# Thirty-five extra series of single-pass products, read from different places in memory, behind the last expert product

## The chip, the cores and the metric

The kernel runs on one core of a Trainium2 chip. The metric is the device time of one execution in microseconds (us); lower is better. A profile is one execution recorded by the hardware profiler; its span runs from the first to the last instruction.

## What is computed

A gated linear attention feeds a small mixture of four experts, all in float32.

```python
# attention: q, k, v, alpha are (4, 8, 768, 48)
for t in range(S):
    state = alpha[:, :, t, :, None] * state + np.einsum('bhd,bhe->bhde', k[:, :, t], v[:, :, t])
    y[:, :, t] = np.einsum('bhd,bhde->bhe', q[:, :, t], state)
# bridge: x = y as (3072, 384)
# experts: w1 (4, 384, 1024), w2 (4, 1024, 384)
p = domain_probs / (domain_probs.sum(-1, keepdims=True) + 1e-09)
for e in range(E):
    h = np.maximum(x @ w1[e], 0.0)
    out += p[:, e:e + 1] * (h @ w2[e])
```

## The kernel before

The 3072 rows of x are 24 blocks of 128 rows. They are worked in groups: the first of two blocks, five of four blocks, the last of two. Attention makes the blocks of a group while TensorE does the expert products of an earlier one. The order of all work is written by hand: `deal` gives attention steps due times, `advance` and `between` call them out between products, and nothing is reordered afterwards. The `for` loop over `tasks` at the end calls `up` (x times w1, rectified) and `down` (that times w2) for each group and expert. The last two groups are done expert by expert together, so the last task is the last group, of 256 rows, with expert 3.

Exact float32 products take several passes through TensorE, so from the second group on most products are split. A number is written as a coarse part and finer parts in the type float32r, and a product is three products of these parts, each of a single pass. `x_part` (`up`, line 555) gives the moving operand of 512 columns, 256 in the last group; `down` (line 648) moves 384 columns of w2. In every one of these products the stationary operand has 128 rows and 128 columns.

A split piece of w1 or w2 is a tile of 128 partitions by 3 parts by 768 float32r numbers, 9,216 bytes in a partition (`wts`, names `w1` and `w2`; `NQ` = 4 buffers for `w2`). `wt[1][i]` is piece i of w2, and `first_piece(gi, e)` is the number of the first of the four pieces of an expert. They come from DRAM in `load_piece` (line 194), on SP's queue, ahead of need.

Accumulated sums stand in banks of PSUM. `one`, `two` and `ops` have one tag, `g`, with four buffers: a new one may be begun when the engine that read the buffer's last content is done. In `add_up` (line 677) VectorE scales a finished `ops` and adds it to the block's `acc`; of the last expert, the store of a block is queued on SP and ScalarE (line 688), behind that sum. After the loop the last stores are issued and the kernel closes: SP waits for all of it, and the engines meet once more.

The constants that the change uses are P = 128, NT = 512, DM = 384, KC = 3 (blocks of 128 in 384) and QF = 256.

Of the kernel before, what the change touches and what calls it, by code (L numbers as in the profile page):

```python
# [10 lines left out]
F32 = mybir.dt.float32  # L11
# [9 lines left out]
def kernel(  # L21
# [37 lines left out]
    nc = tc.nc  # L59

    B, H, S, D = q.shape
    E, DM, F = moe_w1.shape
    P = 128
# [5 lines left out]
    KC = DM // P  # L69
    FCH = F // P  # L70
    NT = B * P
    NQ = 4
    QF = F // NQ
# [11 lines left out]
    n = np.arange(QUAD)[None, :]  # L85
# [9 lines left out]
    ps = ctx.enter_context(tc.tile_pool(name="ps", bufs=2, space=bass.MemoryType.PSUM))  # L95
# [37 lines left out]
    def raw(u, nm):  # L133
        return values[u % 2] if nm == "v" else apart[nm] if u == 1 else early[nm]

    xTs = {}
    xraws = {}
    hidden = {}
# [39 lines left out]
    wt = ({}, {})  # L178
# [38 lines left out]
    def split_piece(l, i):  # L217
        whole = wt[l][i]
        w = wts.tile([P, 3, KC * QF], F32R, name=f"w{l + 1}", bufs=AHEAD if l == 0 else NQ)
        top, low, dif = (w[:, part] for part in range(3))  # L220

        nc.scalar.activation(out=top, in_=whole, func=ACT.Copy, scale=TRIM)
        yield
        nc.scalar.activation(out=dif, in_=whole, func=ACT.Copy, scale=TRIM * 4096)
        yield
        nc.vector.scalar_tensor_tensor(out=low, in0=whole, scalar=4096.0, in1=dif.bitcast(F32),
                                       op0=ALU.mult, op1=ALU.subtract)
        nc.vector.tensor_sub(dif, low.bitcast(F32), top.bitcast(F32))
        nc.gpsimd.dma_start(out=kept[l][i % (E * NQ)], in_=w.bitcast(F32))
        if l == 0:  # L230
            del wt[0][i]
        elif split2(1, *divmod(i - E * NQ, NQ)):
            wt[1][i] = w

    def background():


        for piece in list(splitting):
            if next(piece, splitting) is splitting:
                splitting.remove(piece)  # L240
        if making and len(splitting) < 4:
            splitting.append(making.popleft())
            next(splitting[-1])
# [356 lines left out]
    def make_dif(top, low, dif):  # L600
        nc.vector.scalar_tensor_tensor(out=dif, in0=top.bitcast(F32), scalar=1 / 4096.0,  # L601
                                       in1=low.bitcast(F32), op0=ALU.mult, op1=ALU.subtract)
# [5 lines left out]
    def down(gi, e, slots, between):  # L608


        first = first_piece(gi, e)
        in_parts = [fc for fc in range(FCH) if split2(gi, e, fc // FPQ)]
        whole = [fc for fc in range(FCH) if fc not in in_parts]
        if slots[0] == 0 and makes[1](gi, e):
            making.extend(split_piece(1, first + k) for k in range(NQ) if not split2(gi, e, k))
        if slots[0] == 0 and makes[0](gi, e) and 0 < e < E - 1:
            making.extend(split_piece(0, first + k) for k in range(2, NQ))


        pairs = [slots[k:k + 2] for k in range(0, len(slots), 2)]  # L620
        sides = [[((0, 1), in_parts[:-2]), ((0, 1), in_parts[-2:])], [((3,), whole), ((2,), in_parts)]]
        turns = [(side, pair) for pair in pairs for side in range(2)] if whole else \
            [(side, pair) for side in range(2) for pair in pairs]
        steps = [(side, slot, part, fc) for side, pair in turns
                 for parts, tiles in sides[side] for part in parts for slot in pair for fc in tiles]
        begins = {key: n for n, key in reversed([*enumerate(step[:2] for step in steps)])}
        ends = {step[:2]: n for n, step in enumerate(steps)}
        sums = {}
        for n, (side, slot, part, fc) in enumerate(steps):
            c, f = divmod(fc, FPQ)  # L630
            advance(cost(1, gi, e) * len(slots) / len(steps))
            while between and n >= between[0][0] * len(steps):
                between.popleft()[1]()
            if n and n % (len(steps) // (2 * len(slots))) == 0:
                background()
            if later and n % (len(steps) // 12 - 1) == len(steps) // 12 - 2:
                make_dif(*later.popleft())
            at = (side, slot)
            if n == begins[at]:
                sums[at] = ps.tile([P, DM], F32, name="ops", tag="g", bufs=4)  # L640
            h = hidden[c][:, :, f, slot * P:(slot + 1) * P]
            if part < 3:
                w = wt[1][first + c].rearrange("p t (c d) -> p t c d", d=DM)[:, part, f]
                h = h[:, part]
            else:
                w = wt[1][first + c].rearrange("p (c d) -> p c d", d=DM)[:, f]
                h = h[:, 2].bitcast(F32)
            nc.tensor.matmul(sums[at], lhsT=h, rhs=w, start=(n == begins[at]), stop=(n == ends[at]))  # L648
            if n == ends[at]:
                add_up(gi, e, slot, side, sums.pop(at))  # L650
        while between:
            between.popleft()[1]()
        background()
        if slots[-1] == len(groups[gi]) - 1 and gi != LAST - 1:
            while makes[1](gi, e) and (making or splitting):
                background()

            for c in range(NQ):
                del wt[1][first + c]
                if c < NQ // 2 or gi == LAST:  # L660
                    load_piece(1, first + NQ + c)
                else:
                    late.append(first + NQ + c)

    def add_up(gi, e, slot, kind, part):

        cb, b = groups[gi][slot]
        at = b * NCB + cb
        if e == 0 and (kind == 0 or not split2(gi, e)):
            accs[cb, b] = hid.tile([P, DM], F32, name="acc", bufs=B) if gi < LAST else \  # L670
                work.tile([P, NP * P], F32, name="QT")[:, :DM]
        acc = accs[cb, b]
        scale = (p_fine if kind == 0 else p_all)[:, at, e:e + 1]
        if e == 0 and (kind == 0 or not split2(gi, e)):
            nc.scalar.activation(out=acc, in_=part, func=ACT.Copy, scale=scale)
        else:
            nc.vector.scalar_tensor_tensor(out=acc, in0=part, scalar=scale, in1=acc,  # L677
                                           op0=ALU.mult, op1=ALU.add)
        if kind == 0:
            return  # L680
        if e == E - 1:
            del accs[cb, b]
            row = b * S + cb * P

            queues = (nc.sync, nc.scalar) if gi == LAST else (nc.gpsimd,)
            for i, queue in enumerate(queues):
                rows = slice(P // len(queues) * i, P // len(queues) * (i + 1))
                stores.append(lambda queue=queue, rows=rows: queue.dma_start(
                    out=out[row:row + P, :][rows], in_=acc[rows]))
# [3 lines left out]
    def cost(layer, gi, e):  # L693
        n = len(groups[gi]) / 4
        if layer == 0:
            return 2.1 * n if split1(gi, e) else 2.6 * n
        return 4.1 if gi > 1 else 4.7 if split2(gi, e) else 5.4
# [50 lines left out]
    def advance(spent):  # L748
        nonlocal clock
        clock += spent  # L750
        while waiting and clock >= waiting[0][0]:
            next(waiting.popleft()[2], None)

    with tc.manual_schedule():
# [38 lines left out]
        for fc in range(FCH):  # L793
            up(0, 0, fc, slice(0, 1))
            advance(cost(0, 0, 0) / 2)
        down(0, 0, [0], deque())
        while waiting:
            next(waiting.popleft()[2], None)
# [4 lines left out]
        for (gi, e), after in zip(tasks, [*tasks[1:], (None, None)]):  # L803
# [6 lines left out]
            for k, slots in enumerate(turns):  # L810

                between = deque()
                if after[1] == 0:

                    for step, at in enumerate((0.0, 0.3, 0.42, 0.54) if gi == 0 else
                                              (0.0, 0.6, 0.7, 0.78)):
                        at = at * len(turns) - k
# [3 lines left out]
        while stores:  # L821
            stores.popleft()()


# [1 line left out]
_INS = ['q', 'k', 'v', 'alpha', 'moe_domain_probs', 'moe_w1', 'moe_w2']  # L826
# [24 lines left out]
```

## Time and profile before

| What | Value |
|---|---|
| Time, median of 2 runs | 1051.29 us (1050.86 and 1051.72) |
| Time of the profiled execution | 1051.34 us |
| Its span, first to last instruction | 1049.6 us |
| What lies outside the span (1051.34 less 1049.57) | 1.77 us |
| Granted TensorE clock | 1.000 |
| TensorE matmul records | 8554 |
| VectorE, ScalarE busy | 74%, 54% |
| GpSimd busy | 4% |

PE is TensorE, PEld its weight loads, DVE VectorE, ACT ScalarE, POOL GpSimd, SP SyncE. Matmuls are pipelined: a record of one runs from its start to its modelled end and overlaps the next, so what a product costs in a stream is the step from one start to the next and not the length of its record. L555 is line 555 of the kernel before.

### The profile page before, as it was taken

How to read it: one execution, taken by the hardware profiler on the slowest of the kernel's cores; microseconds unless marked ns; L12 is line 12 of the kernel's file. 1: busy time of each engine (PE TensorE's matmuls, PEld its weight loads, DVE VectorE, ACT ScalarE, POOL GpSimd, SP SyncE). 2: the span in 40 equal slices, each digit the busy share in tenths (PEclk: the TensorE clock that was granted, in tenths of full speed). 3: DMA queues.
4: the chain of work that ended last, by engine and by line, in shares of the span. 5: the costliest groups of instructions: out<-in, count | busy, mean ns of one | idle time of the engine just before them, and what ended most of it. 6: DMA issues, size and time to landing. Idle time of an engine off the chain costs nothing.

```text
span 1049.6 us, 21621 instructions
## 1 busy us (share of the span) xinstructions
PE 1032.5 (98%) x8554; PEld 898.8 (86%) x8554; DVE 778.2 (74%) x1620; ACT 565.6 (54%) x1195; POOL 37.9 (4%) x81
## 2 busy tenths in 40 slices
PE   8899999999999999999999999999999999999998
PEld 8777777687787899898898998898988989898998
DVE  5578787668879868778877777977887875656565
ACT  4787877585666546446446436565464453323232
POOL 3000010000001000000000000000000000000000
PEclk9999999999999999999999999999999999999999
DMA  9397789887868948768669559577595454444531
GB/s 208 92 327 253 220 302 366 305 337 240 285 241 278 384 153 300 288 194 301 255 214 338 184 209 376 185 257 277 162 352 196 166 211 180 181 186 175 209 153 46
DMA packets 145493, 251.65 MB, mean 240 GB/s; under 512 B 107089, under 2 KB 121809, under 8 KB 122865
## 3 DMA queue, kind: packets, MB, share of 16 engines
q1 hardware_dynamic: 138928, 207.88, 57.9%
q0 software_dynamic: 6016, 42.08, 10.1%
q8 instruction: 67, 1.10, 0.4%
q10 hardware_dynamic: 448, 0.32, 0.1%
q14 instruction: 34, 0.27, 0.1%
HBM read 207.79 MB, written 42.47 MB: 238 GB/s over the span
## 4 chain that ended last, share of the span: by engine, by line
PE 86%; DVE 5%; ACT 5%; DMA 2%; issue 2%; POOL 0%; SPq 0%; ACTq 0%; DVEq 0%; POOLq 0%
PE ops L648 35%; PE one L555 23%; PE two L555 11%; PE sc L344 6%; PE yps L439 3%; PE tp L266 3%; PE one L547 2%; ACT qb L317 2%; PE sps L474 1%; PE far L399 1%; DMA w<-kept 1%; DVE near L354 1%; DMA rq<-in_q_dram 1%; PE idle L780 1%; DVE hT L601 1%
## 5 line engine op out<-in xcount | busy, mean ns | idle before, releaser
L648 PE MATMUL ops<-w,hT 128*128 128x384 f32 x1872 | 342.7, 339 | 0.2 <-DVE hT L601 0.2
L648 PEld LDWEIGHTS ops<-w,hT 128*128 128x128 f32 x1872 | 322.6, 188 | 4.0 <-ACT t L566 0.6
L555 PE MATMUL one<-xT,w 128*128 128x512 f32 x960 | 251.8, 398 | 0.8 <-DMA w<-kept 0.4
L555 PEld LDWEIGHTS one<-xT,w 128*128 128x128 f32 x960 | 176.1, 188 | 38.8 <-ACT t L566 1.2
L566 ACT ACTIVATE t<-one 128x512 f32<-128x512 f32 (+1 forms) x192 | 106.7, 556 | 175.8 <-PE one L555 170.2
L317 ACT COPY qb<-QT 64x256 f32<-64x256 f32 x336 | 136.7, 407 | 59.0 <-DVE QT L324 30.6
L595 DVE SCALAR_TENSOR_TENSOR hT<-t,hT 128x512 fp32r<-128x512 f32 (+1 forms) x172 | 110.3, 641 | 63.3 <-ACT hT L593 62.0
L568 DVE TENSOR_TENSOR t<-t,two 128x512 f32<-128x512 f32 (+1 forms) x172 | 109.2, 635 | 53.5 <-PE two L555 31.7
L593 ACT ACTIVATE hT<-t 128x512 fp32r<-128x512 f32 (+1 forms) x172 | 101.8, 592 | 86.8 <-DVE t L568 86.2
L555 PE MATMUL two<-xT,w 128*128 128x512 f32 x480 | 136.5, 393 | 0.1
L555 PEld LDWEIGHTS two<-xT,w 128*128 128x128 f32 x480 | 90.0, 188 | 20.5 <-DVE acc L677 0.9
L648 PE MATMUL ops<-hT 128*128 128x384 f32 x288 | 100.6, 491 | 0.3 <-DVE acc L677 0.3
L601 DVE SCALAR_TENSOR_TENSOR hT<-hT 128x512 fp32r<-128x512 f32 (+1 forms) x172 | 100.6, 633 | 0.0
L354 DVE COPY_PREDICATED near<-masks,sc 128x256 f32<-128x256 uint8 x144 | 77.0, 535 | 22.2 <-PE sc L344 19.2
L324 DVE TENSOR_TENSOR QT<-QT,dec 128x256 f32<-128x256 f32 x144 | 61.0, 423 | 38.9 <-ACT qb L317 38.4
L344 PEld LDWEIGHTS sc<-qb,KT 128*64 128x64 f32 x2304 | 72.7, 138 | 9.0 <-issue 4.8
L344 PE MATMUL sc<-qb,KT 128*64 128x64 f32 x2304 | 77.2, 223 | 2.6 <-ACT qb L317 2.6
L648 PEld LDWEIGHTS ops<-hT 128*128 128x128 f32 x288 | 52.1, 190 | 29.9 <-DVE acc L677 0.6
L677 DVE SCALAR_TENSOR_TENSOR acc<-ops,p_all,acc 128x384 f32<-128x384 f32 x82 | 49.7, 614 | 27.2 <-PE ops L648 26.3
L336 ACT COPY KT<-KT 128x256 f32<-128x256 f32 x138 | 57.5, 417 | 5.1 <-PE sc L344 1.9
L337 DVE TENSOR_TENSOR KT<-KT,dec 128x256 f32<-128x256 f32 x144 | 60.1, 417 | 0.0
L547 PE MATMUL one<-xT,w 128*128 128x256 f32 (+1 forms) x240 | 46.2, 340 | 0.6 <-ACT xT L452 0.6
(90 smaller groups left out, 954.4 us busy)
## 6 DMA issues: line engine op xcount, KB each, us to landing
w<-kept SPq DMA_DIRECT2D x144, 1152.0 KB, 8.2
kept<-w POOLq DMA_DIRECT2D x32, 1152.0 KB, 6.7
hT<-in_moe_w_dram SPq DMA_DIRECT2D x32, 384.0 KB, 6.1
w<-in_moe_w_dram SPq DMA_DIRECT2D x16, 384.0 KB, 6.1
rv<-in_v_dram SPq DMA_DIRECT2D x24, 192.0 KB, 7.3
ra<-in_alpha_dram SPq DMA_DIRECT2D x23, 192.0 KB, 6.1
rk<-in_k_dram SPq DMA_DIRECT2D x23, 192.0 KB, 5.8
rq<-in_q_dram SPq DMA_DIRECT2D x23, 192.0 KB, 5.8
```

The costliest lines, as they stand in the source:

```text
L317: nc.scalar.copy(out=qb[rows, :, i, :].rearrange("p a (b r) -> p a b r", r=m), in_=qv[rows])
L324: nc.vector.tensor_mul(qv, qv, spread(dv[:, :, :, 0], m))
L344: nc.tensor.matmul(out[HALF * s:HALF * (s + 1), 2 * p:2 * p + 2, :], lhsT=KTs[li][:, p, HALF * s:HALF * (s + 1)], rhs=qbs[li][:, p, :, QUA ...
L354: nc.vector.copy_predicated(near.rearrange("p a (b two r) -> p a b two r", two=2, r=m)[:, :, :, 1, :], mk.unsqueeze(1).broadcast_to([P, H, ...
L547: nc.tensor.matmul(one, lhsT=w[:, kc], rhs=xraws[gi][:, kc, lo:hi], start=(kc == 0), stop=(kc == KC - 1))
L555: nc.tensor.matmul(out, lhsT=w[:, part, kc], rhs=x_part(gi, part, kc), start=(part == terms[0] and kc == 0), stop=(part == terms[-1] and k ...
L566: nc.scalar.activation(out=t, in_=one, func=ACT.Copy, scale=FINE)
L568: nc.vector.tensor_add(t, t, two)
L593: nc.scalar.activation(out=top, in_=x, func=ACT.Relu, scale=TRIM)
L595: nc.vector.scalar_tensor_tensor(out=low, in0=x, scalar=0.0, in1=top.bitcast(F32), op0=ALU.max, op1=ALU.subtract)
L601: nc.vector.scalar_tensor_tensor(out=dif, in0=top.bitcast(F32), scalar=1 / 4096.0, in1=low.bitcast(F32), op0=ALU.mult, op1=ALU.subtract)
L648: nc.tensor.matmul(sums[at], lhsT=h, rhs=w, start=(n == begins[at]), stop=(n == ends[at]))
```

## The change

The two first w2 tiles of the expert in hand are remembered in `down`. After the loop and after the last stores are queued, TensorE does 35 series of 13 products with them: the first tile is the stationary side (`still`), the second the moving side (`moved`), each seen as one row of 2,304 numbers in a partition. A series accumulates in one bank (`seen`, tag `g`), and nothing reads it. `begin` is where in the moving tile the series starts, in bytes; `gap` is the distance of its three moving operands, and `weights` are the starts of its stationary operands, both in numbers of four bytes. With `more` = 24 both sides start 96 bytes further on.

```diff
@@ at the head of the kernel
+    last_used = []
     xTs = {}
@@ down
         first = first_piece(gi, e)
+        last_used[:] = [wt[1][first], wt[1][first + 1]]
@@ at the end
         while stores:
             stores.popleft()()
 
+        still, moved = (t.rearrange("p t x -> p (t x)") for t in last_used)
+
+        def series(n, gap, weights, begin, times=13):
+            seen = ps.tile([P, NT], F32, name="seen", tag="g", bufs=4)[:, :n]
+            for k in range(times):
+                at = begin // 4 + gap * (k % 3)
+                w = weights[k % len(weights)]
+                nc.tensor.matmul(seen, lhsT=still[:, w:w + P], rhs=moved[:, at:at + n],
+                                 start=k == 0, stop=k == times - 1)
+
+        for more in (0, 24):
+            first_kind = [more + KC * QF * part + QF * kc for part in range(3) for kc in range(KC)]
+            for diff in (*range(0, 128, 16), 192, 320, 448, 4, 8, 68) if not more else (0, 32, 64, 96):
+                series(NT, NT, first_kind, 4 * more + diff)
+            if not more:
+                for diff in range(0, 128, 16):
+                    series(NT // 2, NT // 2, first_kind, diff)
+                for diff in (*range(0, 128, 16), 320):
+                    series(DM, DM, [0, NT, P, NT + P, 2 * P, NT + 2 * P], diff)
```

## The prediction

> **What bounds the kernel now.** The page's head and its first part come first:
>
> ```profile
> span 1049.6 us, 21621 instructions
> PE 1032.5 (98%) x8554; PEld 898.8 (86%) x8554; DVE 778.2 (74%) x1620; ACT 565.6 (54%) x1195; POOL 37.9 (4%) x81
> ```
>
> TensorE is busy for 98% of the span, at a granted clock of 1.000. What is put behind its last product can be hidden by no wait of its own; the only cover is what now runs after TensorE is done. The chain of waits, asked for the end of the run, shows how little that is (start us, length us, what):
>
> ```profile
> 1036.57 0.35 PE two L555 x3
> 1036.93 8.55 PE ops L648 x48
> 1045.48 0.02 issue
> 1045.50 0.62 DVE QT L677
> ```
>
> The chain ends with VectorE's last sum at 1046.12. The timeline of the same place has what follows, and the DMA view gives the issues' median time to landing:
>
> ```profile
> 1045.13 0.34 PE L648 MATMUL ops<-w,hT 128*128 128x384 f32 x1
> 1045.50 0.62 DVE L677 SCALAR_TENSOR_TENSOR QT<-ops,p_all,QT 128x384 f32<-128x384 f32 x1 [0.77 <-PE ops L648]
> 1046.15 0.48 SPq L688 DMA_DIRECT2D out_dram<-QT  x1
> 1046.15 0.51 ACTq L688 DMA_DIRECT2D out_dram<-QT  x1
> ```
>
> ```profile
> out_dram<-QT SPq DMA_DIRECT2D x2, 96.0 KB, 2.2
> out_dram<-QT ACTq DMA_DIRECT2D x2, 96.0 KB, 2.4
> ```
>
> The last stores land at about 1046.15 + 2.4 = 1048.55, and the remaining 1.0 us to 1049.57 is the close.
>
> Now the pace. The change adds only single-pass products, with moving operands of 512, 256 and 384 columns; the kernel has all three shapes in undisturbed stretches. These are two windows of the chain:
>
> ```profile
> 903.70 1.37 PE one L555 x6
> 905.07 0.69 PE two L555 x3
> 905.76 1.37 PE one L555 x6
> ...
> 909.88 16.64 PE ops L648 x96
> ```
>
> ```profile
> 928.68 0.72 PE one L555 x6
> 929.40 0.36 PE two L555 x3
> 929.76 0.72 PE one L555 x6
> ```
>
> Nine products of 512 columns take 905.76 - 903.70 = 2.06 us, a step of 228.9 ns. Nine of 256 columns take 929.76 - 928.68 = 1.08 us, a step of 120.0 ns. The 96 of 384 columns step by 16.64 / 96 = 173.3 ns. These are prices with the switch of weights in them, and with the switch of the bank: `one` and `two` lie in different banks. The record's length is something else:
>
> ```profile
> L648 PE MATMUL ops<-w,hT 128*128 128x384 f32 x1872 | 342.7, 339 | 0.2 <-DVE hT L601 0.2
> L555 PE MATMUL two<-xT,w 128*128 128x512 f32 x480 | 136.5, 393 | 0.1
> L648 PEld LDWEIGHTS ops<-w,hT 128*128 128x128 f32 x1872 | 322.6, 188 | 4.0 <-ACT t L566 0.6
> ```
>
> A product has a record of 339 ns and its weight load one of 188 ns, yet the next starts after 173.3 ns: load, stream and drain of neighbours overlap.
>
> **The change part by part.** Remembering two tiles is bookkeeping while the program is made and issues nothing. The built program confirms it: the first 6,261 products, their order and addresses are as before, other engines get nothing new, and the 455 products stand behind. No DMA is added or moved.
>
> Counting: 14 series with `more` = 0 and 4 with 24 are of 512 columns, 18 x 13 = 234 products; 8 x 13 = 104 have 256 columns; 9 x 13 = 117 have 384. At the steps above:
> - 234 x 228.9 ns = 53.6 us
> - 104 x 120.0 ns = 12.5 us
> - 117 x 173.3 ns = 20.3 us
>
> Together 86.3 us, all on the path, since TensorE has nothing else left and closing waits for it.
>
> Waits in the series: the first four each take a bank whose `ops` VectorE must have read. The last of those sums ends at 1046.12, and the fourth series is due three series later, at 1045.30 + 3 x 2.98 = 1054.2. Later series wait for TensorE's own series four before, long done. I price both at nothing. If that cover failed, a stop for TensorE's own drain would cost about one record less a step, 339 - 173 = 166 ns, and 35 of them 5.8 us. Nothing is queued behind those waits but further series. Operands need no load: both tiles were used by the last expert.
>
> The end: the last old product starts at 1045.13, so the first new one can start one step later, at 1045.30. The last new one starts at 1045.30 + 86.3 - 0.23 = 1131.4 and its record of 0.39 us ends at 1131.8. VectorE's last sum and the stores (to 1048.55) now lie beside the series. With the same 1.0 us of close (between 0 and the 3.45 us that follow VectorE's sum today) the span is 1132.8 us, and with the 1.77 us outside it the time is 1134.6 us. That is against the profiled 1051.34, which is 0.05 above the median; I say 1135.
>
> The uncertain price is the place in memory. In the built program the moving tile starts at byte 50,080 of a partition and the stationary one at 59,296, a distance of 9,216, which is 18 x 512. So modulo 512 the distance of the two operands is minus the byte offset that the series asks for. Before, that distance, stationary less moving, was always 192 for the 512-column products, 448 for the 384-column ones and 0 for the 256-column ones. Only three of the 35 series repeat the place of their own shape (offset 320 at 512 columns, 64 at 384, 0 at 256); 32 series, 416 products, are at places that the trace does not price. What it does say: the three steps fit 0.417 ns per column plus a fixed part, (173.3 - 120.0) / 128 = 0.416, and 120.0 - 256 x 0.417 = 13.3 ns fixed at a distance of 0, 173.3 - 160.0 = 13.3 at 448, 228.9 - 213.3 = 15.6 at 192. Three unlike places have nearly the same fixed part, so I take the rows as they are for the rest. Below, the fixed part can at best vanish: 416 x 13.5 ns = 5.6 us less, 1129. Above, it could grow; a load that overlaps nothing is the far end, 416 x 188 ns = 78 us more, 1213. I stay near the rows because load and stream overlap at all three.
>
> Two rules of the Trainium skill bear on this. The page "TensorE: Matmul & The Clock Gate", section "Back-to-back issue gap", gives an isolated gap of columns / 2.4 + 2.5 ns, an estimate of 80.9 us for the 455 products and 1129 in all; the row of 228.9 ns for 512 columns is above its 215.8, and the row decides. The same page, in Part 3, lets a weight load overlap running products only when it is for other rows of the array, which would put 188 ns on each product and end near 1220; the 96 full-array products at 173.3 ns speak against it.
>
> **The rivals.**
> - Places collide (slower still). Weights for the next product are read while this one streams; if their places decide whether the reads meet, the fixed part of 13.3 ns is a mild case. For it: that fixed part exists, and single steps of 512 columns vary by some ns. Against it: it is the same at three distances. Doubled on 416 products it adds 5.5 us, 1140; four times as large 16.6 us, 1151. Middle 1146.
> - Places help: the fixed part vanishes at most of the new places, 1129. Against it: the same three rows.
> - The products aren't run, or cost next to nothing, as nobody reads the bank. This one ends on the other side, not slower: 1051. The mechanism is a program cut of unread work between build and chip; it decides if a product costs under (21 + 3) / 455 = 53 ns, 21 us being 2% of the time and 3 us the cover at the end. Against it: the built program has all 455, and the shortest new shape steps by 120 ns.
>
> **How the numbers follow.** The rows as they are: 0.70, 1135, own range 1132 to 1138. Places collide: 0.18, 1140 to 1151 and rarely beyond. Places help: 0.08, about 1129. Not run: 0.025; a load that overlaps nothing 0.015. The range from 1129 to 1148 takes the first case, the larger part of the second and the third, and leaves under 2 in 10 out. A change of 2%, 21 us, is about what measurement can tell from none. Slower by over 2% has all but the case of no execution: 0.97; within 2% 0.025, faster 0.005.
>
> **What would show it.** In the changed profile TensorE should have 9,009 matmul records (8554 + 455), a new group with output `seen` in three shapes, and no idle time at a start of a series. The chain should end with about 86 us of `seen`, its steps 229, 120 and 173 ns; the last stores should be issued near 1046 as now. Steps that differ from series to series by their offset alone would show that places count, and gaps between series a wait that I priced at nothing. I am wrong if the mean over the 455 products is outside 177 to 219 ns; 86.3 us is 190.

## The result and the profile after

| | Before | After |
|---|---|---|
| Time, median of 2 runs | 1051.29 us | 1135.02 us (1134.72 and 1135.32) |
| Ratio, with its 95% interval | | 1.0795 (1.0777 to 1.0812) |
| Profiled execution | 1051.34 us | 1134.72 us |
| Its span | 1049.6 us | 1132.9 us |
| TensorE matmul records | 8554 | 9009 |

The change made the kernel 83.7 us slower. The page of the changed kernel opens so:

```profile
span 1132.9 us, 22532 instructions
PE 1119.5 (99%) x9009; PEld 975.3 (86%) x9009; DVE 778.1 (69%) x1620; ACT 565.5 (50%) x1195; POOL 37.9 (3%) x81
```

TensorE has 455 records more and every other engine has what it had: VectorE's busy time is 778.1 us against 778.2. The view of the cores gives the same granted clock as before:

```profile
core 0: 1132.9 us, clock 1.000
```

The groups of TensorE from 1044.8 us on, with shapes kept apart (busy us, mean record, idle before):

```profile
L833 PE MATMUL seen<-w,w 128*128 128x512 f32 x234 | 54.6, 394 | 0.0
L833 PE MATMUL seen<-w,w 128*128 128x384 f32 x117 | 20.6, 337 | 0.0
L833 PE MATMUL seen<-w,w 128*128 128x256 f32 x104 | 12.4, 280 | 0.0
```

All three shapes are there in the number forecast, and none has idle time before it. The chain of waits at the seam (start us, length us, what):

```profile
1036.45 8.55 PE ops L650 x48
1045.00 1.16 PE seen L833 x5
```

TensorE goes from the old products to the new without a gap. The timeline there shows what is now beside them:

```profile
1044.66 0.34 PE L650 MATMUL ops<-w,hT 128*128 128x384 f32 x1
1044.84 5.46 PE L833 MATMUL seen<-w,w 128*128 128x512 f32 x23
...
1045.04 0.62 DVE L679 SCALAR_TENSOR_TENSOR QT<-ops,p_all,QT 128x384 f32<-128x384 f32 x1 [0.77 <-PE ops L650]
1045.69 0.47 SPq L690 DMA_DIRECT2D out_dram<-QT  x1
1045.69 0.51 ACTq L690 DMA_DIRECT2D out_dram<-QT  x1
```

VectorE's last sum and the last stores are issued as they were, and now lie beside the first series. The windows are the four blocks of the change in their order: 14 series of 512 columns, 8 of 256, 9 of 384, 4 of 512. The first figure of a row is its length, and the counts in brackets include records that reach in from a neighbour:

```profile
1044.84:1087.16 42.32, 42.32 (x183) 34.27 (x183) 1.00 0.04 10
1087.16:1099.42 12.26, 12.26 (x106) 12.26 (x105) 1.00 0.00 1
1099.42:1119.82 20.40, 20.40 (x120) 20.40 (x118) 1.00 0.00 1
1119.82:1131.82 12.00, 12.00 (x53) 9.57 (x52) 1.00 0.00 0
```

The series take 42.32 + 12.00 = 54.3 us at 512 columns, 12.3 at 256 and 20.4 at 384, together 87.0 us, or mean steps of 232.1, 117.9 and 174.4 ns.

Within the changed kernel the mean step of a series already differs by offset: 226.8 to 237.0 ns at 512 columns, 113.3 to 119.8 at 256, 173.2 to 176.8 at 384 (each the mean of twelve steps, from the starts of the records). Whether that is the place, and what else the 87 us hold, is what the experiments ask. The edits of the kernels with series are shown against the changed kernel; the last three kernels have no series, and their edits are shown against the kernel before. `...` stands for lines left out.

### The profile page after: what moved, and what is told of

The parts are those of the page before. It is cut to its first block, busy times and chain, and to the rows that moved or that the text cites. A ratio compares the mean times of both kernels' runs of the same rounds, so it can differ in the third digit from the quotient of the medians.

```text
span 1132.9 us, 22532 instructions
## 1 busy us (share of the span) xinstructions
PE 1119.5 (99%) x9009; PEld 975.3 (86%) x9009; DVE 778.1 (69%) x1620; ACT 565.5 (50%) x1195; POOL 37.9 (3%) x81
## 4 chain that ended last, share of the span: by engine, by line
PE 89%; DVE 5%; ACT 3%; issue 1%; DMA 1%; SPq 0%; POOL 0%; ACTq 0%; DVEq 0%; POOLq 0%
PE ops L650 33%; PE one L556 21%; PE two L556 10%; PE seen L833 8%; PE sc L345 5%; PE yps L440 3%; PE tp L267 3%; PE one L548 2%; ACT qb L318 1%; PE sps L475 1%; PE far L400 1%; DVE near L355 1%; DMA rq<-in_q_dram 1%; DVE hT L602 1%; PE idle L782 1%
## 5 line engine op out<-in xcount | busy, mean ns | idle before, releaser
L833 PE MATMUL seen<-w,w 128*128 128x512 f32 (+2 forms) x455 | 87.1, 353 | 0.0
L833 PEld LDWEIGHTS seen<-w,w 128*128 128x128 f32 x455 | 76.7, 188 | 10.2
```

The source lines that it names most:

```text
L833: nc.tensor.matmul(seen, lhsT=still[:, w:w + P], rhs=moved[:, at:at + n], start=k == 0, stop=k == times - 1)
```

## Is the price per product, or per series?

Edit:

```diff
-        def series(n, gap, weights, begin, times=13):
+        def series(n, gap, weights, begin, times=26):
```

> Each of the 35 series has 26 products instead of 13; nothing else differs from the changed kernel. Theory (the price is per product): the second 13 cost what the first did, about 87.0 us more than the changed kernel, 1222 us. Rival (a good part of the 87 us belongs to the beginning of a series, its new bank and its wait): the added products are cheaper than the first, and the time is well under 1218 us, for instance 1205 us if a fifth of the price belongs to the 35 beginnings.

Measured: 1222.41 us in one run, beside 1051.24 for the kernel before on the same chip. That is 87.4 us above the changed kernel, and the second 455 products cost what the first did. The first start to the last is 173.9 us for 910 products against 86.7 us for 455. Nothing of the price belongs to the beginning of a series.

The next kernel multiplies the beginnings instead. The sums over 13 products are left out, since each product stands alone in its bank.

```diff
-            seen = ps.tile([P, NT], F32, name="seen", tag="g", bufs=4)[:, :n]
             for k in range(times):
+                seen = ps.tile([P, NT], F32, name="seen", tag="g", bufs=4)[:, :n]
...
-                                 start=k == 0, stop=k == times - 1)
+                                 start=True, stop=True)
```

> Each of the 455 products begins a buffer of its own among the four, so that there are 455 waits in place of 35; the sums over 13 products are left out. Theory (such a wait is free, since TensorE's own product four before is long done): the time stays at 1135 us within 2 us, and the steps stay at about 232, 118 and 174 ns. Rival (a wait or a new bank has a price that 35 of them hide): at 20 ns each 455 cost 9 us, 1144 us.

Measured: 1134.32 us, in one run. From the first start to the last are 86.745 us, to the nanosecond what the changed kernel takes, and no step differs by more than 1 ns. A new bank and a wait on TensorE's own product four back are free, 455 times as well as 35 times.

## What if the cover at a beginning is taken away?

One bank for all series, and VectorE copies one column of it after each:

```diff
+        bank = ps.tile([P, NT], F32, name="seen", tag="g", bufs=4)
+        read = tot[:, :1]
...
-            seen = ps.tile([P, NT], F32, name="seen", tag="g", bufs=4)[:, :n]
+            seen = bank[:, :n]
...
+            nc.vector.tensor_copy(out=read, in_=seen[:, :1])
```

> All 35 series use one bank, and VectorE copies one column of it after each, so each series must wait for the one before to end and to be read. Theory (the four buffers are the cover that makes the beginnings free): each of 34 beginnings now costs TensorE's drain, 166 ns or more, and VectorE's short read behind it, some 300 to 500 ns together, so 10 to 17 us and 1145 to 1152 us, with idle TensorE before each series put down to VectorE. Rival (products of neighbouring series overlap whatever the bank): 1135 to 1137 us.

Measured: 1154.14 us in one run, 19 us above the changed kernel and 2 above the forecast. The waits from 1045 us on (us in all, times, longest):

```profile
DVE tot L838 <- PE seen L836: 98.7, 35, 3.5
PEld seen L836 <- DVE tot L838: 20.4, 34, 0.7
PE seen L836 <- DVE tot L838: 8.6, 34, 0.3
```

Both the product and its weight load wait for VectorE, 34 times. One such beginning in the timeline:

```profile
1046.32 3.14 PE L836 MATMUL seen<-w,w 128*128 128x512 f32 x13
...
1049.50 0.16 DVE L838 COPY tot<-seen 128x1 f32<-128x1 f32 x1 [2.37 <-PE seen L836]
1049.71 2.84 PEld L836 LDWEIGHTS seen<-w,w 128*128 128x128 f32 x13 [0.68 <-DVE tot L838]
1049.71 3.28 PE L836 MATMUL seen<-w,w 128*128 128x512 f32 x13 [0.25 <-DVE tot L838]
```

The series ends, VectorE's copy takes 0.16 us, and load and first product begin together at 1049.71. The step over the boundary is 413 ns longer on the mean of 34, and the step after it 106 ns longer (339 in place of 232 ns at 512 columns). The likely reason of the second is the load: in the changed kernel a weight load starts 188 ns before its product on the mean, and at these beginnings 7 ns before it. With some 3 ns on later steps that is 522 ns a beginning, 34 x 0.522 = 17.8 us, the difference between 104.50 and 86.745 us from first start to last. Of the rest, about 1.5 us is that this execution reached the series later (1046.32 against 1044.84). The four buffers are a real cover. This kernel takes them away and adds a reader at once, so it prices the two together; what TensorE's own drain alone would cost, which the prediction put at 166 ns, no run separates.

## What does the place cost?

96 series in place of the 35, at every multiple of 16 bytes below 512 (`third_kind` is the list of six starts that the change uses at 384 columns):

```diff
...
+        for diff in range(0, 512, 16):
+            series(NT, NT, first_kind, diff)
+        for diff in range(0, 512, 16):
+            series(NT // 2, NT // 2, first_kind, diff)
+        for diff in range(0, 512, 16):
+            series(DM, DM, third_kind, diff)
```

> In place of the 35 series there are 96, for each of the three widths one at every multiple of 16 bytes from 0 to 496, so 416 products of each width. Theory (the distance of the operands shifts a step by a few ns and repeats after 256 bytes): the mean step of a series is 226 to 234 ns at 512 columns, 113 to 121 at 256 and 173 to 177 at 384; the two series of a width whose offsets differ by 256 agree within 1 ns, those that differ by 128 do not. In all 416 x (0.231 + 0.118 + 0.1745) = 218 us of series and 1266 us. Rival (the differences between the series of the changed kernel are chance, or belong to their order in time): series 256 bytes apart differ as much as any two. Second rival (places collide): some of the offsets that were not tried before step by 20 ns or more above the rest.

Measured: 1266.58 us in one run. Four of the 256-column series, at the offsets 0, 64, 256 and 320, as windows:

```profile
1141.83:1143.39 1.56, 1.56 (x15) 1.56 (x13) 1.00 0.00 0
1148.00:1149.47 1.47, 1.47 (x15) 1.47 (x14) 1.00 0.00 0
1166.34:1167.89 1.55, 1.55 (x16) 1.55 (x15) 1.00 0.00 0
1172.50:1173.97 1.47, 1.47 (x16) 1.47 (x14) 1.00 0.00 0
```

Thirteen products take 1.56, 1.47, 1.55 and 1.47 us: 0 and 256 agree, 64 and 320 agree, and the two pairs differ. Over all offsets, mean steps in ns from the starts of the records:

| Columns | Shortest | Longest | Mean | Series 256 bytes apart differ by, on the mean | Series 128 bytes apart |
|---|---|---|---|---|---|
| 512 | 228.7 (256) | 234.9 (208) | 232.5 | 0.09 | 1.9 |
| 256 | 113.3 (64) | 119.8 (0) | 117.9 | 0.07 | 0.9 |
| 384 | 173.2 (32, 192) | 179.1 (496) | 175.2 | 0.08 | 2.4 |

The largest difference at 256 bytes is 1.1 ns, and in each width it is the series at offset 0, which follows another width. So the differences aren't chance: they repeat with 256 bytes. And none of the untried offsets is far from the rest, so the rival in which places collide finds nothing here.

These series move only one operand, so its address alone could be what counts. The four last series of the changed kernel, in which both operands lie 96 bytes further on, speak for the distance: at the distances of the offsets 0, 32, 64 and 96 they step by 226.8, 233.7, 230.0 and 233.2 ns, and the first series at these distances by 229.7, 233.1, 230.0 and 234.2. By the moving operand's address the first of them would be like offset 96, 234.2 ns, and the third like offset 160, 233.2 here. This is shown for 512 columns alone.

Two kernels then put all series of a width at one offset. The edit is that of the first, near; the second, far, has 4, 0 and 240 where this has 0, 64 and 0.

```diff
-                series(NT, NT, first_kind, 4 * more + diff)
+                series(NT, NT, first_kind, 4 * more + 0)
...
-                    series(NT // 2, NT // 2, first_kind, diff)
+                    series(NT // 2, NT // 2, first_kind, 64)
...
-                series(DM, DM, [0, NT, P, NT + P, 2 * P, NT + 2 * P], diff)
+                series(DM, DM, [0, NT, P, NT + P, 2 * P, NT + 2 * P], 0)
```

> The 35 series keep their number, widths and order, but all of a width use the offset with the shortest step: 0 bytes at 512 columns, 64 at 256, 0 at 384. Theory (the distance of the operands alone makes the differences between series, and they are small): 234 x 228.7 + 104 x 113.3 + 117 x 173.4 ns = 85.6 us of series against 87.0, so 1133.6 us. Rival (the differences are chance, or come with a series' place in the order): 1135.0 us. Second rival (places matter more when a place is kept): more than 4 us from 1135.

> As before, but all series of a width use the offset with the longest step: 4 bytes at 512 columns, 0 at 256, 240 at 384. Theory: 234 x 237.0 + 104 x 119.8 + 117 x 179.0 ns = 88.9 us of series against 87.0, so 1136.9 us, 3.3 us above the kernel with the short steps. Rivals as there: 1135.0 us, or more than 4 us from it.

Measured: 1133.51 us (four runs, 1132.91 to 1133.85) and 1137.41 us (1136.80 to 1137.50); as ratios to the kernel before 1.0783 (1.0765 to 1.0801) and 1.0818 (1.0802 to 1.0834). The runs of the two don't overlap. The kernels differ in the places alone, and the difference is 3.9 us, 0.3% of the time; in the two traces the series account for 3.4 us of it (85.46 and 88.89 us from first start to last). The near kernel has 512-column series with and without the 96 bytes on both sides: 13 of 14 without and three of four with them step by 226.7 ns, the other two begin the change or follow another width. So the distance stands against the address once more. Both totals came as forecast, the near one by two errors that cancel. At 512 columns the step was 227.0 ns where 228.7 was taken. At 256 columns and offset 64 it was 117.8, not 113.3, though the same width at the same offset had given 113.3 in the changed kernel, with a bank for each product and among the 96 series. The kernel with series of 26 products shows it as well, with the offsets in their old order: 117.8 at offset 64, and at offset 112 a step that goes from 116.0 in its first twelve steps to 113.3 in its last twelve. The distance is thus not all that sets a step: what ran before counts too. How was not tried.

## What is the fixed part?

The prediction split a step into 0.417 ns per column and a fixed 13.3 ns, and one rival rested on weight reads that meet the stream. Here the load gets shorter:

```diff
...
-                nc.tensor.matmul(seen, lhsT=still[:, w:w + P], rhs=moved[:, at:at + n],
+                nc.tensor.matmul(seen, lhsT=still[:, w:w + cols], rhs=moved[:, at:at + n],
...
+        for n, weights in ((NT, first_kind), (DM, third_kind), (NT // 2, first_kind)):
+            for diff in (0, 64, 96):
+                for cols in (P, P - 32, P // 2, P // 4):
+                    series(n, n, weights, diff, cols)
```

> In place of the 35 series there are 36: widths 512, 384 and 256, each at the offsets 0, 64 and 96 bytes, each with 128, 96, 64 and 32 stationary columns, so that the weight load reads as many columns. Theory (the fixed part of a step, about 13 ns, is the reads of the next weights meeting the stream): the fixed part falls with the columns, to about 7 ns at 64 and 3 ns at 32, so steps of about 220 and 217 ns at 512 columns. Rival (a constant cost of changing from one product to the next): the steps stay at 227 to 233, 173 to 177 and 113 to 120 ns whatever the stationary columns are.

Measured: 1129.59 us in one run, with 156 products of each width. The loads did get shorter (busy us, mean of one):

```profile
L833 PEld LDWEIGHTS seen<-w,w 128*128 128x128 f32 x117 | 19.0, 188 | 2.2
L833 PEld LDWEIGHTS seen<-w,w 128*96 128x96 f32 x117 | 17.2, 161 | 3.1
L833 PEld LDWEIGHTS seen<-w,w 128*64 128x64 f32 x117 | 15.0, 134 | 5.2
L833 PEld LDWEIGHTS seen<-w,w 128*32 128x32 f32 x117 | 12.6, 108 | 7.5
```

The steps did not follow. These are windows of whole series at offset 0: 512 columns with 128 and with 32 stationary columns, then 384 columns with the same two:

```profile
1045.37:1048.35 2.98, 2.98 (x13) 2.41 (x14) 1.00 0.50 132
1054.32:1057.34 3.02, 3.02 (x15) 1.50 (x14) 1.00 0.00 0
1081.42:1083.70 2.28, 2.28 (x14) 2.27 (x13) 1.00 0.00 0
1088.23:1090.49 2.26, 2.26 (x14) 1.46 (x13) 1.00 0.00 0
```

A load that reads a quarter of the columns leaves 13 products at 2.98 and 3.02 us of 512 columns, and at 2.28 and 2.26 us of 384. My theory of colliding reads falls at these widths. Only at 256 columns did the load matter, from 119.9 to 113.3 ns at offset 0 and from 119.7 to 117.4 at offset 96, and not at offset 64, which had 113.3 all along. Is what remains a constant, then? The last kernel of this kind varies the width, with 128 and with 32 stationary columns:

```diff
...
+        for n in (128, 192, 256, 320, 384, 448, 512):
+            for diff in (0, 64):
+                for cols in (P, P // 4):
+                    series(n, NT, first_kind, diff, cols)
```

> In place of the 35 series there are 28: widths 128, 192, 256, 320, 384, 448 and 512, each at offsets 0 and 64 bytes, each with 128 and 32 stationary columns. What is told apart is the part of a step that goes beyond 0.4167 ns per column, now that fewer stationary columns left it as it was at 512 and 384 columns. Theory (a constant per product, 13.3 ns): the steps with 32 stationary columns are 67, 93, 120, 147, 173, 200 and 227 ns. Rival (the stream itself is slower by a sixteenth, so 0.4427 ns per column and nothing fixed): 57, 85, 113, 142, 170, 198 and 227 ns. With 128 stationary columns either may be longer where the load, some 107 ns of columns, is longer than the stream: at 128 and 192 columns.

Measured: 1102.60 us in one run. Mean of the last nine full steps of a series in ns (offset 0, offset 64), and, with 32 stationary columns, the part beyond 0.4167 ns per column (the prediction's 0.417):

| Columns | 32 stationary | Beyond | 128 stationary |
|---|---|---|---|
| 128 | 60.2, 59.6 | 6 to 7 | 111.7, 111.4 |
| 192 | 88.6, 89.6 | 9 to 10 | 111.4, 111.7 |
| 256 | 117.8, 113.7 | 7 to 11 | 119.4, 117.8 |
| 320 | 143.4, 145.4 | 10 to 12 | 146.7, 146.4 |
| 384 | 173.1, 175.8 | 13 to 16 | 173.6, 173.2 |
| 448 | 202.1, 206.7 | 15 to 20 | 203.1, 200.0 |
| 512 | 231.7, 231.8 | 18 | 226.7, 228.9 |

It is not a constant: it grows with the columns, 7 ns at 128 and 18 at 512. Neither forecast holds: the constant is 7 ns too much at 128 columns and 5 too little at 512, and all steps lie above the rival's 0.4427 ns per column, by up to 6%. A line through the two ends, 0.4475 ns per column and 2.6 ns (an estimate from these rows), passes within 4 ns of all between. With 128 stationary columns these two places hardly show the growth (13 ns at 320, 13 and 16 at 512); the means over the 32 places do, with 11.2, 15.2 and 19.1 ns beyond at 256, 384 and 512. With 128 stationary columns there is also a floor of about 111.5 ns; with 32 the products of 128 and 192 columns take 60 and 89 ns, so it comes with the stationary columns, and the longer load is the likely reason. What makes the part grow with the width stays open.

## Does a better place help the kernel itself?

Three kernels without series move operands of the kernel before by unused memory, so that the distance of the 512-column products goes from 192 to 0, or that of the 256-column products from 0 to 448, or both; the padding behind keeps all other distances modulo 512. The edit for both:

```diff
-    PAD = 32
+    PAD = 112
...
         QT = work.tile([P, NP, P], F32, name="QT")
+        if u == 0:
+            work.tile([P, 16], F32, name="gap1", bufs=1)
...
+                    work.tile([P, 32], F32, name="gap2", bufs=1)
                     xTs[gi] = work.tile([P, 3, KC, NT], F32R, name="xT", bufs=1)
```

> The kernel before, without any series; 192 bytes of unused memory ahead of the moving operand of the 512-column products and as many more behind it as make 512, so that these 1440 products have the distance 0 modulo 512 in place of 192, and all others keep theirs. Theory (the steps measured behind the last product hold within the kernel): 1440 x (229.4 - 227.0) ns = 3.5 us less than before, about 1047.8 us. Rival (other engines' traffic, which was absent behind the last product, hides so small a difference): 1051.3 us within 0.5.

> The kernel before, without any series; 64 bytes of unused memory ahead of the tiles that hold the moving operand of the 256-column products, and 448 behind them, so that these 288 products have the distance 448 modulo 512 in place of 0, and the other single-pass products keep theirs. Theory: 288 x (120.0 - 113.3) ns = 1.9 us less if the short steps of the changed kernel's series come, 288 x (120.0 - 117.8) = 0.6 us if those of the run with near places do, so 1049.4 to 1050.7 us. Rival (no difference within the kernel): 1051.3 us within 0.5.

> The kernel before, without any series, with both distances changed as in the two other kernels. Theory: the two gains add, 4.1 to 5.4 us, 1046 to 1047.2 us, faster than both the kernel before and the changed one. Rival: 1051.3 us within 0.5.

| Kernel | Median of 11 runs, us | Ratio to before, with its 95% interval |
|---|---|---|
| 512-column operands moved | 1049.85 | 0.9986 (0.9977 to 0.9995) |
| 256-column operands moved | 1050.96 | 0.9997 (0.9988 to 1.0006) |
| Both moved | 1049.51 | 0.9986 (0.9977 to 0.9995) |

The kernel before had 1051.18 us (27 runs) beside them. Moving the 512-column operands is a gain of 1.3 us. It is small but clear of the interval, and a third of what the series promised. In the profiled executions the mean undisturbed step of these products went from 229.4 to 228.6 ns, not to 227.0; 1440 x 0.8 = 1.2 us is about the gain. The 256-column step went from 119.8 to 117.7 ns, 0.6 us by count, which these runs can't tell from nothing. The version with both has the lowest median, 1049.51 us. It is faster than the kernel before by 0.14%, and so than the changed one; these runs don't tell it from the first of the three.

## Why the prediction was right

- **Nothing hides it.** Right. TensorE was the bound at the end, and the series stand in the chain in full.
- **Count times step.** 86.3 us forecast, 87.0 measured, a mean of 191 ns where 190 was forecast. By width: 53.6 against 54.3, 12.5 against 12.3, 20.3 against 20.4. The term that was off most is the 512-column step, taken as 228.9 ns from the one place that the kernel used, while the mean over the places that the change visits is 232.1. That is 3.2 ns x 234 = 0.75 us. By chance the two rows lay at the ends of what places do: 228.9 is near the shortest at 512 columns (228.7 to 234.9), and 120.0 is as long as the longest at 256 (113.3 to 119.8).
- **Waits at nothing.** Right, shown by the bank for each product, which took the same time to the nanosecond. The price that I put on a lost cover, 166 ns for TensorE's drain, was not tested by itself: with one bank and a reader a beginning cost 522 ns, which has the reader, its signals and the late weight load in it.
- **The end.** The first new product was forecast at 1045.30 and came at 1044.84, as the execution was some 0.5 us ahead at the seam (the last 48 old products start at 1036.45 against 1036.93). That and the 0.7 us above nearly cancel. The last record ends at 1131.98 and the span at 1132.94, so the close is 0.96 us where 1.0 was taken, and 1134.6 became 1134.72. An agreement of 0.1 us is partly luck; one of a microsecond is not.
- **Places.** The bounds were wide and the rows were the right choice. At 512 columns places shift a step by 6.2 ns among the 16-byte offsets, and by about 10.7 between the kernels with all series near and all far (227.0 and 237.8); the rival in which places collide, with 13 ns or more on every unseen place, found no such case. But the reason given, one fixed part at three unlike places, was weak. By the period of 256 bytes two of the three distances, 192 and 448, are one place. And the part is not fixed: over the 32 places it is 11.2 ns at 256 columns and 19.1 at 512. That the three rows came out at 13.3, 13.3 and 15.6 ns was a coincidence of their places; the forecast used the steps themselves, and did not suffer.

## What to carry to other kernels

On an engine that is busy to the end, added work costs its count times the step between starts, read from an undisturbed stretch of the same shape; the record's length would have given 1.7 to 2.4 times as much here. Ask of each cover at a boundary (a spare bank, a weight load ahead) what it hides, since losing it costs more than the wait alone. A difference of a few ns that shows behind the last product, with nothing else running, shrank to a third inside the kernel, so a gain of that kind has to be run where it is meant to be used.

## What was not expected of the hardware

- The step of single-pass products depends on the distance of their two operands in memory; at 512 columns it stayed when both were moved by 96 bytes (226.7 ns and 226.7). The step repeats every 256 bytes to 0.1 ns on the mean, and spans 6 ns in 230. It isn't a function of that distance alone: 256 columns at offset 64 stepped by 113.3 ns in four kernels and by 117.8 in three others.
- Their pace is slower than 0.4167 ns per column by an amount that grows with the columns, 7 ns at 128 and 18 at 512 (32 stationary columns).
- Moving operands that start 4 bytes on made the longest steps at 512 columns, 237.0 ns in one series and 237.8 over all 18 of a kernel.
- With 128 stationary columns the step didn't fall below about 111.5 ns: 128 and 192 moving columns cost the same, where 32 stationary columns gave 60 and 89 ns.
